# Strassen sums of a weight matrix made by accumulating DMAs instead of VectorE, in an FNet + gMLP block

## The chip, the cores and the metric

The kernel runs on one core of one Trainium2 chip. The metric is the device time of one execution in microseconds. Before the change three runs took 945.85 to 947.27 us, with a median of 946.61 us.

## The reference

The block is an FNet layer followed by a gMLP layer, on one sequence of 2048 rows and 512 columns, all in fp32. Cut to what matters:

```python
h = layernorm(x) * (1 + ca) + sa
a, b = h @ hid_re.T, h @ hid_im.T                   # 512 x 512
x = x + ga * (seq_re @ a - seq_im @ b)              # 2048 x 2048, twice
h = layernorm(x) * (1 + cb) + sb
z = gelu(h @ w_in)                                  # 512 x 1792
z1, z2 = z[..., :896], layernorm(z[..., 896:])
g = w_sp @ z2 + b_sp                                # 2048 x 2048
x = x + gb * ((z1 * g) @ w_out)                     # 896 x 512
```

The vectors `sa` to `gb` come from `silu(c) @ w_mod`. The change concerns the product with `w_sp` alone.

## The kernel before, in words

Every fp32 operand is split into a high and a low part, and every product is made as three TensorE matmuls (`matmul3`, lines 95 to 97: high by high, high by low, low by high). ScalarE makes a high part with one copy (`prep_hi`, line 256, tile `ah`), VectorE makes the low part with one subtraction (`prep_lo`, line 263, tile `al`). A unit `n` of the program is one 128 x 512 piece of a left-hand matrix, which TensorE multiplies in 12 matmuls. The pieces come in blocks of 512 x 512, four units to a block: SyncE issues four DMAs that load a block into `stage` (line 154, two buffers), and VectorE transposes it (line 227, tile `t`).

The program has these stages. Stage one is units 0 to 127: the two 2048 x 2048 DFT products, with the four groups of `mm_y` (tile `yp`) between the units, each of which ends in work on VectorE, GpSimd and ScalarE (`post_y`, `norm_y`, `post_h`). Then come 28 units for z1 (`N2` is 128, `N3` is 156), 16 units for z2, and 112 units (from `N4` on) for the product with `w_sp`; last the output product (`op`).

The product with `w_sp` is a Strassen-Winograd product with seven forms instead of eight, in the order 1, 6, 7, 4, 5, 3, 2 (`PROD`). Three of them read quarters of `w_sp` as they stand; the forms 5, 6, 7 and 3 read four sums of the quarters A11, A12, A21 and A22: S1 = A21 + A22, S2 = S1 - A11, S3 = A11 - A21 and S4 = A12 - S2. These are made ahead of time, piece by piece, during stage one and the z stages. A piece is loaded by SyncE into `sj` (line 756), VectorE makes the four sums in place (lines 761, 762, 765, 766), and GpSimd's queue stores them to `s_d` in HBM (line 769), from where the product's units load them like any other block (line 160).

The order on each engine is the order in which the program is written: `at(n, f, ...)` puts a call into the list of unit `n`, and `run(n)` calls the list after the unit's matmuls were written. Each engine, and each engine's DMA queue, runs its instructions in that order and waits at the first whose inputs or buffers are not ready. Line 1111 on places the pieces: 16 pieces of 128 rows by 512 columns in each of the four quarters, eight of them every five units from unit 85 on, each with its sums four and five units after its load; the other eight in the z stages. `sj` has two buffers in stage one (`spre0`, opened at unit 84) and four in the z stages. Just before unit 128 the pool that holds `spre0` is closed, and tiles of the z1 stage are put in its place, among them the weight sum `wt` (line 657).

GpSimd also holds, in the same queue, the loads of `xr` (line 544), the stores of `x_d` and `h_d` (lines 570 and 581) and the small arithmetic of the layer norm (lines 107, 108, 115), whose result ScalarE waits for in `norm_y` (line 119).

Of the kernel before, what the change touches and what calls it, by code (L numbers as in the profile page):

```python
# [19 lines left out]
def fnet_gmlp_kernel(  # L20
# [32 lines left out]
    nc = tc.nc  # L53
    S, D = x.shape[1:]
    F2 = w_in.shape[1]
    FH = F2 // 2
    Q = 512
# [18 lines left out]
    dram = ctx.enter_context(tc.tile_pool(name="dram", bufs=1, space=bass.MemoryType.DRAM))  # L76
    ctx.enter_context(tc.manual_schedule())

    def bank(k, name):
# [3 lines left out]
    h2_d = [dram.tile([Q, D], F32, name=f"h2_d{t}") for t in range(NQ)]  # L83
    z1_d = [dram.tile([NF, P, Q], F32, name=f"z1_d{t}") for t in range(NQ)]
    S_OF = {5: 1, 6: 2, 7: 3, 3: 4}
    s_d = {(m, r, g): dram.tile([Q, Q], F32, name=f"s_d{m}_{r}{g}")
           for m in range(1, 5) for r in range(2) for g in range(2)}
    def split(hi, lo, src):

        nc.scalar.activation(hi, src, AF.Copy)  # L90
        nc.vector.tensor_tensor(lo, src, hi.bitcast(F32), op=ALU.subtract)
# [31 lines left out]
    def at(n, f, *a):  # L123
        fill.setdefault(n, []).append((f, a))
# [6 lines left out]
    def quad(a, r, k):  # L131
        return a[r * Q:(r + 1) * Q, k * Q:(k + 1) * Q]
# [6 lines left out]
    N2 = 4 * len(src)  # L139
# [21 lines left out]

    def load(b):
        if b < len(src):
            stage[b] = blocks.tile([P, 16, P], F32, tag="stage", bufs=2, name=f"stage{b}")
            load_block(stage[b], src[b])
        elif b < len(src) + NQ * len(PROD):
            i, gh = divmod(b - len(src), NQ)
            g, h = divmod(gh, 2)
            p = PROD[i]
            stage[b] = blocks.tile([P, 2, 16, 64], F32, tag="stage", bufs=2, name=f"stage{b}")  # L170
            for r in range(2):
                load_half(stage[b][:, r], s_d[S_OF[p], r, g] if p in S_OF else
                          quad(w_sp, r + (2 if p == 4 else 0), g + (0 if p == 1 else 2)), h)

    def squares(dst, block, k):
# [26 lines left out]
    def turn_one(n, b0=0, b1=16):  # L202

        if b0 == 0:
            slot(n)
        squares(T[n][:, 32 * b0:32 * b1], stage[n % 2][:, b0:b1], n // 2)
        if n // 2 == 3 and b1 == 16:
            stage.pop(n % 2)
            if n % 2:
                load(3)  # L210
# [405 lines left out]
    def turn_z(t):  # L616
        b, q = N2 // 4 + t, t // 2
        if t == 1:
            ht = wpool[0].tile([P, 4, Q], F32, tag="wih", bufs=1, name="hz1")
        else:  # L620
            ht = spre[-1].tile([P, 4, Q], F32, tag="sj", bufs=4, name=f"hz{t}")
        st = stage.pop(b)
        for m in range(2):
            nc.vector.transpose(ht[:, 2 * m:2 * m + 2].rearrange("p k (b i) -> p k b i", i=32),
                                st[:, :, 64 * m:64 * m + 64].rearrange("p b (k i) -> p k b i", k=2))
        if t > 1:
            load(b + 2)
        if t % 2:
            RAW[q, 7], RAW[q, 4] = ht[:, :2], ht[:, 2:]
        else:  # L630
            RAW[q, 1] = RAW[q, 6] = ht[:, :2]
            RAW[q, 2] = RAW[q, 3] = ht[:, 2:]
# [114 lines left out]

    SJ = {}

    def load_s(r, g, b):  # L750

        SJ[r, g, b] = spre[-1].tile([P, 4, Q], F32, tag="sj", bufs=4 if len(spre) > 1 else 2, name=f"sj{r}{g}{b}")
        for i in range(2):
            v = w_sp.rearrange("(i r) (j c) -> i r j c", i=2, j=2)[i]
            o = r * Q + b * P
            nc.sync.dma_start(SJ[r, g, b][:, 2 * i:2 * i + 2], v[o:o + P][:, :, g * Q:(g + 1) * Q])

    def sum_s(r, g, b, first):
        a11, a12, a21, a22 = [SJ[r, g, b][:, i] for i in range(4)]
        if first:  # L760
            nc.vector.tensor_tensor(a22, a21, a22, op=ALU.add)  # L761
            nc.vector.tensor_tensor(a21, a11, a21, op=ALU.subtract)
            done = (1, a22), (3, a21)
        else:
            nc.vector.tensor_tensor(a11, a22, a11, op=ALU.subtract)
            nc.vector.tensor_tensor(a12, a12, a11, op=ALU.subtract)
            done = (2, a11), (4, a12)
        for m, a in done:
            nc.gpsimd.dma_start(s_d[m, r, g][b * P:(b + 1) * P, :], a)  # L769


    GW, UT, X2, OP, G, BH, BL = {}, {}, {}, {}, {}, {}, {}
# [12 lines left out]
    def b_of(p, k):  # L785
        return Z[k + 8 if p in (3, 2) else k][:, F2_ if p in (7, 5, 3) else F1]

    def hi_b(p, k):
        w = b_of(p, k).shape[-1]
        BH[p, k] = bpool[0].tile([P, Q], F32R, tag="bh", bufs=3, name=f"bh{p}_{k}")  # L790
        nc.scalar.activation(BH[p, k][:, :w], b_of(p, k), AF.Copy)  # L791

    def lo_b(p, k):
        w = b_of(p, k).shape[-1]
        BL[p, k] = bpool[0].tile([P, Q], F32R, tag="bl", bufs=3, name=f"bl{p}_{k}")
        nc.vector.tensor_tensor(BL[p, k][:, :w], b_of(p, k), BH[p, k][:, :w].bitcast(F32), op=ALU.subtract)

    def mm_w(n):
        i, m = divmod(n - N4, 4 * NQ)
# [204 lines left out]
    for s, n in ((8, 10), (9, 10)):  # L1004
        m = n + (s == 9)
# [23 lines left out]
    for j, turn, weigh, row, fold, hi in ((0, (25, 26, 27, 28), (29, 29, 30, 30), 26, (34, 34, 35, 36), (38, 35, 36, 37)),  # L1029
# [8 lines left out]
        n = weigh[3] + (3 if j == 0 else 1)  # L1038
# [21 lines left out]
    for t in range(NQ):  # L1060
        n = 8 * NQ * (t + 1)
# [35 lines left out]
    wpool, zpool, zrow, bpool, spre, gpool = [], [], [], [], [], []  # L1097
# [10 lines left out]
        spre.append(hp.enter_context(pool("spre0")))  # L1108

    at(84, change_q)  # L1110
    for i, u in enumerate((r, g, b) for g in range(2) for b in range(4) for r in range(2)):
        n = 85 + 5 * i if i < 8 else N2 + (13, 15, 28, 29, 31, 33, 35, 37)[i - 8]
        m = n + (4 if i < 8 or i > 9 else (9, 13)[i - 8])
        at(n, load_s, *u)
        at(m, sum_s, *u, True)
        at(m + 1, sum_s, *u, False)
    for n in range(N2):
        prep(n)
        mm_a(n)
# [25 lines left out]
    for i, p in enumerate(PROD):  # L1145
        for k in range(8):
            n = NB[p] + 2 * k
            at(n - 5, hi_b, p, k)
            at(n - 4, lo_b, p, k)
            if p == 1:  # L1150
                at(n + 3, sum_t23, k)
            if p == 4:
                at(n - 6, sum_t14, k)
# [33 lines left out]
    for f in range(NF):  # L1187
        n = NB[6] + 3 * f
# [66 lines left out]
```

## Time and profile before

| what | value |
|---|---|
| median of three runs | 946.61 us |
| span of the profiled execution, first to last instruction | 945.0 us |
| TensorE (PE) busy | 938.0 us, 99% of the span |
| VectorE (DVE) busy | 707.0 us, 75% |
| ScalarE (ACT) busy | 386.9 us, 41% |
| GpSimd (POOL) busy | 177.4 us, 19% |
| mean granted TensorE clock | 1.000 |
| bytes moved by DMA | 161.79 MB, 171 GB/s over the span |

The times in the profile are microseconds from the start of the span. The span is 1.6 us below the median of the runs, so a number that is worked out in the span is carried to the runs as a difference. SPq and ACTq are the queues (sequencers) of SyncE and ScalarE. In a row of a group, "x16 | 10.9, 680" means 16 instructions, 10.9 us in all, 680 ns each; what follows the second bar is the engine's idle time just before them and what ended it.

### The profile page before, as it was taken

How to read it: one execution, taken by the hardware profiler on the slowest of the kernel's cores; microseconds unless marked ns; L12 is line 12 of the kernel's file. 1: busy time of each engine (PE TensorE's matmuls, PEld its weight loads, DVE VectorE, ACT ScalarE, POOL GpSimd, SP SyncE). 2: the span in 40 equal slices, each digit the busy share in tenths (PEclk: the TensorE clock that was granted, in tenths of full speed). 3: DMA queues.
4: the chain of work that ended last, by engine and by line, in shares of the span. 5: the costliest groups of instructions: out<-in, count | busy, mean ns of one | idle time of the engine just before them, and what ended most of it. 6: DMA issues, size and time to landing. Idle time of an engine off the chain costs nothing.

```text
span 945.0 us, 12296 instructions
## 1 busy us (share of the span) xinstructions
PE 938.0 (99%) x4158; PEld 780.9 (83%) x4158; DVE 707.0 (75%) x1048; ACT 386.9 (41%) x670; POOL 177.4 (19%) x333
## 2 busy tenths in 40 slices
PE   8999999999999999999999999999999999999998
PEld 6878888888888888888888999888888888888886
DVE  7789957775765657767978587877688688885872
ACT  3685424232232222322876356544544444331221
POOL 1430000221631145122323265200000000000000
PEclk9999999999999999999999999999999999999999
DMA  8998653577668965996398985555554456833541
GB/s 194 222 214 165 130 134 90 146 197 158 134 101 197 281 208 150 279 281 141 95 344 282 326 267 160 149 114 134 124 134 90 106 117 141 205 107 117 198 155 59
DMA packets 253230, 161.79 MB, mean 171 GB/s; under 512 B 134576, under 2 KB 222896, under 8 KB 253040
## 3 DMA queue, kind: packets, MB, share of 16 engines
q1 hardware_dynamic: 238544, 120.62, 53.7%
q0 software_dynamic: 12272, 39.61, 12.3%
q10 hardware_dynamic: 2352, 0.79, 0.3%
q8 instruction: 32, 0.52, 0.3%
q14 instruction: 30, 0.25, 0.1%
HBM read 124.26 MB, written 36.71 MB: 170 GB/s over the span
## 4 chain that ended last, share of the span: by engine, by line
PE 94%; DMA 2%; SPq 1%; issue 1%; POOL 1%; DVE 0%; ACT 0%; ACTq 0%; DVEq 0%; POOLq 0%
PE gp L96 11%; PE gp L97 11%; PE gp L95 11%; PE gw L95 10%; PE gw L96 10%; PE gw L97 10%; PE yp L97 3%; PE yp L96 3%; PE yp L95 3%; PE z2p L96 3%; PE z2p L95 3%; PE z2p L97 3%; PE op L97 3%; PE op L95 3%; PE op L96 3%; PE z1p L96 1%
## 5 line engine op out<-in xcount | busy, mean ns | idle before, releaser
L256 ACT ACTIVATE ah<-t 128x512 fp32r<-128x512 f32 x263 | 164.4, 627 | 310.2 <-PE gp L97 181.0
L263 DVE TENSOR_TENSOR al<-t,ah 128x512 fp32r<-128x512 f32 x264 | 179.9, 685 | 133.4 <-PE gp L96 59.8
L96 PE MATMUL gp<-al,hh 128*128 128x512 f32 x480 | 186.8, 389 | 1.2 <-DVE al L263 1.2
L97 PE MATMUL gp<-ah,hl 128*128 128x512 f32 x480 | 186.8, 389 | 0.0
L95 PE MATMUL gp<-ah,hh 128*128 128x512 f32 x480 | 186.7, 389 | 0.0
L97 PE MATMUL gw<-ah,bl 128*128 128x512 f32 x400 | 155.6, 389 | 0.0
L96 PE MATMUL gw<-al,bh 128*128 128x512 f32 x400 | 155.6, 389 | 0.0
L95 PE MATMUL gw<-ah,bh 128*128 128x512 f32 x400 | 155.6, 389 | 0.0
L96 PEld LDWEIGHTS gp<-al,hh 128*128 128x128 f32 x480 | 90.1, 188 | 20.4 <-DVE al L263 1.6
L95 PEld LDWEIGHTS gp<-ah,hh 128*128 128x128 f32 x480 | 90.1, 188 | 18.7
L97 PEld LDWEIGHTS gp<-ah,hl 128*128 128x128 f32 x480 | 90.1, 188 | 18.8 <-DVE hl L448 0.2
L97 PEld LDWEIGHTS gw<-ah,bl 128*128 128x128 f32 x400 | 75.1, 188 | 15.7
L95 PEld LDWEIGHTS gw<-ah,bh 128*128 128x128 f32 x400 | 75.1, 188 | 15.5
L96 PEld LDWEIGHTS gw<-al,bh 128*128 128x128 f32 x400 | 75.1, 188 | 15.5
L227 DVE STREAM_TRANSPOSE t<-stage 128x1024 f32<-128x1024 f32 x62 | 76.7, 1238 | 8.7 <-DMA stage<-in_A_dft_seq_re_dram 8.6
L221 DVE STREAM_TRANSPOSE t<-stage 128x1024 f32<-128x1024 f32 x56 | 69.3, 1238 | 0.1
L791 ACT ACTIVATE bh<-z 128x512 fp32r<-128x512 f32 (+1 forms) x56 | 32.8, 586 | 65.7 <-PE gw L96 65.7
L769 POOL DMA_DIRECT2D s_d<-sj x64 | 35.1, 550 | 107.5 <-DVE sj L761 80.7
L95 PE MATMUL yp<-hth,gh 128*128 128x512 f32 x128 | 49.8, 389 | 0.0
L96 PE MATMUL yp<-htl,gh 128*128 128x512 f32 x128 | 49.8, 389 | 0.0
L97 PE MATMUL yp<-hth,gl 128*128 128x512 f32 x128 | 49.8, 389 | 0.0
L96 PE MATMUL z2p<-wil,ah 128*128 128x448 f32 x128 | 46.7, 365 | 0.0
(210 smaller groups left out, 1448.0 us busy)
## 6 DMA issues: line engine op xcount, KB each, us to landing
sj<-in_B_w_sp_dram SPq DMA_DIRECT2D x32, 512.0 KB, 8.3
s_d<-sj POOLq DMA_DIRECT2D x64, 256.0 KB, 4.1
stage<-s_d SPq DMA_DIRECT2D x128, 128.0 KB, 2.9
stage<-in_A_dft_seq_re_dram SPq DMA_DIRECT2D x60, 256.0 KB, 5.4
stage<-in_A_dft_seq_im_dram SPq DMA_DIRECT2D x60, 256.0 KB, 5.9
stage<-in_B_w_sp_dram SPq DMA_DIRECT2D x96, 128.0 KB, 3.1
stage<-h_d SPq DMA_DIRECT2D x32, 256.0 KB, 6.4
xr<-in_A_x_dram POOLq DMA_DIRECT2D x16, 256.0 KB, 4.3
```

What stands on the lines that cost most here:

```text
L95: nc.tensor.matmul(acc, ah, bh, start=first, stop=False, skip_group_check=go_on)
L96: nc.tensor.matmul(acc, ah, bl, start=False, stop=False, skip_group_check=go_on)
L97: nc.tensor.matmul(acc, al, bh, start=False, stop=last, skip_group_check=go_on)
L221: nc.vector.transpose(t.rearrange("p r (b i) -> p r b i", i=32), st[:, :, :, 16 * k:16 * k + 32])
L227: nc.vector.transpose(t.rearrange("p k (b i) -> p k b i", i=32), st[:, :, 32 * k:32 * k + 64].rearrange("p b (k i) -> p k b i", k=2))
L256: nc.scalar.activation(AH[n], source(n), AF.Copy)
L263: nc.vector.tensor_tensor(AL[n], source(n), AH[n].bitcast(F32), op=ALU.subtract)
L769: nc.gpsimd.dma_start(s_d[m, r, g][b * P:(b + 1) * P, :], a)
L791: nc.scalar.activation(BH[p, k][:, :w], b_of(p, k), AF.Copy)
```

## The change

The four sums are no longer made by VectorE. The pieces become 8 strips of 128 rows by 2048 columns in each half of `w_sp`, and every sum is made by DMAs, some of which add what they carry to what lies at their destination:

1. SyncE loads the strip's lower rows (A21 and A22) into `sj`, 1 MB, and copies A12 from `w_sp` in HBM to the place of S4 in HBM, 512 KB (`load_s`).
2. ScalarE negates both halves of `sj`; GpSimd's queue stores -A21 to the place of S1 (`negate_s`).
3. GpSimd's queue adds -A22 to S1 in HBM, and adds A11 from HBM to -A21 in `sj`, which becomes S3 (`sum_s1`).
4. It stores S3, and adds S3 to -A22 within `sj`, which becomes -S2 (`sum_s2`).
5. It stores -S2, and adds -S2 to the A12 in the place of S4 (`sum_s4`).

S1 and S2 are held with the opposite sign, so the products 5 and 6 take the negative of their other operand: `hi_b` copies with a scale of -1, and `lo_b` becomes one `scalar_tensor_tensor`. The first six strips are placed every six units from unit 85 on, with their steps four, six, eight and ten units after the load; the last two lie in the z stages.

```diff
-    s_d = {(m, r, g): dram.tile([Q, Q], F32, name=f"s_d{m}_{r}{g}")
-           for m in range(1, 5) for r in range(2) for g in range(2)}
+    s_d = {(m, r): dram.tile([Q, 2 * Q], F32, name=f"s_d{m}_{r}") for m in range(1, 5) for r in range(2)}
...
-    def load_s(r, g, b):
-        SJ[r, g, b] = spre[-1].tile([P, 4, Q], F32, tag="sj", bufs=4 if len(spre) > 1 else 2, name=f"sj{r}{g}{b}")
-        for i in range(2):
-            v = w_sp.rearrange("(i r) (j c) -> i r j c", i=2, j=2)[i]
-            o = r * Q + b * P
-            nc.sync.dma_start(SJ[r, g, b][:, 2 * i:2 * i + 2], v[o:o + P][:, :, g * Q:(g + 1) * Q])
-
-    def sum_s(r, g, b, first):
-        a11, a12, a21, a22 = [SJ[r, g, b][:, i] for i in range(4)]
-        if first:
-            nc.vector.tensor_tensor(a22, a21, a22, op=ALU.add)
-            nc.vector.tensor_tensor(a21, a11, a21, op=ALU.subtract)
-            done = (1, a22), (3, a21)
-        else:
-            nc.vector.tensor_tensor(a11, a22, a11, op=ALU.subtract)
-            nc.vector.tensor_tensor(a12, a12, a11, op=ALU.subtract)
-            done = (2, a11), (4, a12)
-        for m, a in done:
-            nc.gpsimd.dma_start(s_d[m, r, g][b * P:(b + 1) * P, :], a)
+    def s_rows(m, b):
+        return s_d[m, b // 4][b % 4 * P:(b % 4 + 1) * P, :]
+
+    def load_s(b):
+        SJ[b] = spre[-1].tile([P, 2, 2 * Q], F32, tag="sj", bufs=4 if len(spre) > 1 else 2, name=f"sj{b}")
+        nc.sync.dma_start(SJ[b], w_sp[S // 2 + b * P:S // 2 + (b + 1) * P, :].rearrange("p (j c) -> p j c", j=2))
+        nc.sync.dma_start(s_rows(4, b), w_sp[b * P:(b + 1) * P, 2 * Q:])
+
+    def negate_s(b):
+        for j in range(2):
+            nc.scalar.activation(SJ[b][:, j], SJ[b][:, j], AF.Copy, scale=-1.0)
+        nc.gpsimd.dma_start(s_rows(1, b), SJ[b][:, 0])
+
+    def sum_s1(b):
+        nc.gpsimd.dma_start(s_rows(1, b), SJ[b][:, 1], accum_op=ALU.add)
+        nc.gpsimd.dma_start(SJ[b][:, 0], w_sp[b * P:(b + 1) * P, :2 * Q], accum_op=ALU.add)
+
+    def sum_s2(b):
+        nc.gpsimd.dma_start(s_rows(3, b), SJ[b][:, 0])
+        nc.gpsimd.dma_start(SJ[b][:, 1], SJ[b][:, 0], accum_op=ALU.add)
+
+    def sum_s4(b):
+        nc.gpsimd.dma_start(s_rows(2, b), SJ[b][:, 1])
+        nc.gpsimd.dma_start(s_rows(4, b), SJ[b][:, 1], accum_op=ALU.add)
...
-        nc.scalar.activation(BH[p, k][:, :w], b_of(p, k), AF.Copy)
+        nc.scalar.activation(BH[p, k][:, :w], b_of(p, k), AF.Copy, scale=-1.0 if p in (5, 6) else 1.0)
...
-        nc.vector.tensor_tensor(BL[p, k][:, :w], b_of(p, k), BH[p, k][:, :w].bitcast(F32), op=ALU.subtract)
+        hi = BH[p, k][:, :w].bitcast(F32)
+        if p in (5, 6):
+            nc.vector.scalar_tensor_tensor(BL[p, k][:, :w], b_of(p, k), -1.0, hi, op0=ALU.mult, op1=ALU.subtract)
+        else:
+            nc.vector.tensor_tensor(BL[p, k][:, :w], b_of(p, k), hi, op=ALU.subtract)
...
-    for i, u in enumerate((r, g, b) for g in range(2) for b in range(4) for r in range(2)):
-        n = 85 + 5 * i if i < 8 else N2 + (13, 15, 28, 29, 31, 33, 35, 37)[i - 8]
-        m = n + (4 if i < 8 or i > 9 else (9, 13)[i - 8])
-        at(n, load_s, *u)
-        at(m, sum_s, *u, True)
-        at(m + 1, sum_s, *u, False)
+    for b in range(8):
+        n = 85 + 6 * b if b < 6 else N2 + (16, 20)[b - 6]
+        m = n + 4 if b < 6 else N2 + (28, 31)[b - 6]
+        at(n, load_s, b)
+        at(m, negate_s, b)
+        at(m + 2, sum_s1, b)
+        at(m + 4, sum_s2, b)
+        at(m + 6, sum_s4, b)
```

What the change moves is seen best on three queues. On GpSimd, before, from the first piece on: four stores of one piece (`sj_2733` is its buffer), a load of `xr`, and the four stores of the next.

```order
L769 DMA s_d_00_88<-sj_2733 128x512
L769 DMA s_d_00_96<-sj_2733 128x512
L769 DMA s_d_00_92<-sj_2733 128x512
L769 DMA s_d_00_100<-sj_2733 128x512
L544 DMA xr_0_2895<-in_A_x_dram 128x512
L769 DMA s_d_10_90<-sj_2842 128x512
```

The same place now, with the whole of the first strip (`sj_2725`): the rows of lines 765, 766, 770 and 774 are the four that add.

```order
L762 DMA s_d_0_88<-sj_2725 128x1024
L765 DMA s_d_0_88<-sj_2725 128x1024
L766 DMA sj_2725<-in_B_w_sp_dram 128x1024
L543 DMA xr_0_2884<-in_A_x_dram 128x512
L769 DMA s_d_0_92<-sj_2725 128x1024
L770 DMA sj_2725<-sj_2725 128x1024
L773 DMA s_d_0_90<-sj_2725 128x1024
L774 DMA s_d_0_94<-sj_2725 128x1024
L762 DMA s_d_0_88<-sj_2847 128x1024
```

Before, the stores of a piece read only what VectorE had made. Now line 765 adds to what line 762 stored, line 769 and line 770 read what line 766 made, and lines 773 and 774 read what line 770 made: each must wait for an earlier DMA of the same queue to land, and what stands behind it waits with it.

On ScalarE, now, around the negation of the strip with index 5 (`sj_3553`), which is placed at unit 119; before, this place held `ah` rows alone.

```order
L255 ACTIVATE ah_3601<-t_3558 128x512
L255 ACTIVATE ah_3617<-t_3594 128x512
L761 ACTIVATE sj_3553<-sj_3553 128x1024 x2
L255 ACTIVATE ah_3640<-t_3594 128x512
L255 ACTIVATE ah_3656<-t_3638 128x512
```

The row `ah_3640` is the high part for unit 123. ScalarE comes to it only when the strip has been loaded and negated.

On SyncE, now, from the third strip on. Every strip's load is one row of 1 MB and one copy from HBM to HBM of 512 KB, and its place between the loads of `stage` is fixed; before, there were two loads of 512 KB at each such place.

```order
L755 DMA sj_3015<-in_B_w_sp_dram 128x2048
L756 DMA s_d_0_94<-in_B_w_sp_dram 128x1024
L153 DMA stage_3022<-in_A_dft_seq_re_dram 32x16x128 x4
L153 DMA stage_3160<-in_A_dft_seq_im_dram 32x16x128 x4
L755 DMA sj_3229<-in_B_w_sp_dram 128x2048
L756 DMA s_d_0_94<-in_B_w_sp_dram 128x1024
```

The third strip takes the first strip's buffer, so its row waits until the last row of the first strip on GpSimd (line 774) has landed, and the four rows of `stage` behind it wait with it.

More of the change, by code (lines that the diff above doesn't have):

```diff
@@ L171, in load @@
             for r in range(2):
-                load_half(stage[b][:, r], s_d[S_OF[p], r, g] if p in S_OF else
+                load_half(stage[b][:, r], s_d[S_OF[p], r][:, g * Q:(g + 1) * Q] if p in S_OF else
                           quad(w_sp, r + (2 if p == 4 else 0), g + (0 if p == 1 else 2)), h)
```

## The prediction

> **What bounds the kernel now.** I read the engines' totals first, then what TensorE waited for, then the long middle of the span by itself.
>
> ```profile
> span 945.0 us, 12296 instructions
> PE 938.0 (99%) x4158; PEld 780.9 (83%) x4158; DVE 707.0 (75%) x1048; ACT 386.9 (41%) x670; POOL 177.4 (19%) x333
> ...
> engine line waited for: us in total, times, longest us
> PE busyp L349 <- DVE busy L284: 1.5, 1, 1.5
> PE gp L96 <- DVE al L263: 1.2, 1, 1.2
> PE gp L468 <- DVE ah L959: 0.9, 1, 0.9
> ...
> 75.00:925.00 850.00, 850.00 (x3791) 711.16 (x3790) 643.20 (x941) 338.26 (x572) 155.38 (x265) 1.00 0.64 170
> ```
>
> The last row is a window of 850 us: its columns are the length, then busy time and count of PE, PEld, DVE, ACT and POOL, the granted clock, the DMA share and GB/s. TensorE was busy in all 850 us, at a granted clock of 1.00. Its waits in the whole span sum to 3.6 us, all in the first 75 us, which the change does not touch. So between 75 and 925 us no other engine's work costs time as long as it is in time, and VectorE, busy in 643 of these 850 us, holds TensorE up nowhere. A saving on VectorE can therefore give nothing. The whole question is whether the new work is ever late.
>
> **What goes away.** The sums on VectorE:
>
> ```profile
> L766 DVE TENSOR_TENSOR sj<-sj 128x512 f32<-128x512 f32 x16 | 12.0, 753 | 0.6
> L762 DVE TENSOR_TENSOR sj<-sj 128x512 f32<-128x512 f32 x16 | 12.0, 752 | 0.6
> L761 DVE TENSOR_TENSOR sj<-sj 128x512 f32<-128x512 f32 x16 | 10.9, 680 | 1.7 <-DMA sj<-in_B_w_sp_dram 1.7
> L765 DVE TENSOR_TENSOR sj<-sj 128x512 f32<-128x512 f32 x16 | 10.6, 663 | 0.0
> ...
> L528 DVE SCALAR_TENSOR_TENSOR ht<-ht,col,w 128x512 f32<-128x512 f32 x8 | 5.7, 729 | 0.0
> ...
> L796 DVE TENSOR_TENSOR bl<-z,bh 128x512 fp32r<-128x512 f32 x32 | 20.9, 652 | 0.0
> ```
>
> That is 64 instructions and 45.5 us of VectorE, worth 0 us of the span by the window above. The 16 `lo_b` of the products 5 and 6 become another form: the nearest row, 729 ns, against 652 ns makes at most 16 x 0.08 = 1.2 us on an engine with a quarter of its time free, and I take 0.
>
> **What comes onto ScalarE.** Sixteen negations of 128 x 1024. The nearest rows:
>
> ```profile
> L668 ACT ACTIVATE wh<-wraw 128x1024 fp32r<-128x1024 f32 x3 | 3.2, 1056 | 1.9 <-DMA wraw<-in_B_w_in_dram 1.5 <-DVE wraw L657 0.4
> ...
> 401.20 0.63 ACT L256 ACTIVATE ah<-t 128x512 fp32r<-128x512 f32 x1 [2.08 <-PE gp L97]
> 403.93 0.63 ACT L256 ACTIVATE ah<-t 128x512 fp32r<-128x512 f32 x1 [2.10 <-PE gp L97]
> ...
> 412.08 0.63 ACT L256 ACTIVATE ah<-t 128x512 fp32r<-128x512 f32 x1 [2.08 <-PE gp L97]
> ```
>
> 2 x 1.06 = 2.1 us a strip, against idle times of 2.1 us before each `ah`: the work itself is hidden. What is not cheap is the wait in front of it. ScalarE makes `ah` for unit n + 3 at unit n and is let on by TensorE's end of unit n - 1. With the row at 401.20 (unit 119) four units ahead of the row at 412.08, TensorE can go on until 412.1 us with what ScalarE has made before the negation placed at unit 119. After that it stands still until the strip has landed, been negated and the next `ah` (0.63 us) is made.
>
> **What comes onto the DMA engines.** This is the part that can hurt. Before, a piece had a load of 2 x 512 KB and four stores of 256 KB. Its price, and what the DMA engines reach:
>
> ```profile
> sj<-in_B_w_sp_dram SPq DMA_DIRECT2D x32, 512.0 KB, 8.3
> s_d<-sj POOLq DMA_DIRECT2D x64, 256.0 KB, 4.1
> ...
> 300.00:325.00 25.00, 25.00 (x112) 20.70 (x111) 17.95 (x24) 7.97 (x13) 4.79 (x9) 1.00 0.88 273
> 325.00:350.00 25.00, 25.00 (x112) 20.69 (x111) 15.62 (x23) 5.26 (x8) 11.05 (x18) 1.00 0.71 201
> 350.00:375.00 25.00, 25.00 (x112) 20.71 (x111) 14.95 (x23) 4.85 (x8) 9.43 (x15) 1.00 0.69 190
> 375.00:400.00 25.00, 25.00 (x112) 20.71 (x111) 19.99 (x27) 7.98 (x13) 6.59 (x10) 1.00 0.86 259
> 400.00:425.00 25.00, 25.00 (x112) 20.67 (x112) 16.69 (x24) 6.94 (x12) 6.49 (x12) 1.00 0.98 269
> ...
> 475.00:500.00 25.00, 25.00 (x112) 20.71 (x111) 19.51 (x25) 18.20 (x30) 5.37 (x10) 1.00 1.08 351
> ```
>
> In the stretch where the sums are made the DMA engines are busy 0.69 to 0.98 of the time already, at a mean of 238 GB/s. The most that any window shows is 351 GB/s, with a share above 1; I take that as what they can do.
>
> Now the size of a slot. The first sums of the pieces at units 89, 119 and 124 started here:
>
> ```profile
> 298.25 0.69 DVE L761 TENSOR_TENSOR sj<-sj 128x512 f32<-128x512 f32 x1
> ...
> 401.61 0.68 DVE L761 TENSOR_TENSOR sj<-sj 128x512 f32<-128x512 f32 x1
> ...
> 416.37 0.65 DVE L761 TENSOR_TENSOR sj<-sj 128x512 f32<-128x512 f32 x1
> ```
>
> The strips stand six units apart, so 30 units in 103.4 us make 20.7 us a strip. Before, a piece every (416.37 - 298.25) / 7 = 16.9 us moved 1.05 MB in and 1.05 MB out, so 2.6 MB in 20.7 us. All traffic in 20.7 us was 238 x 20.7 = 4.9 MB; what is left for `stage` and the rest is 2.3 MB. Now a strip moves 1.05 MB (load) and eight times 0.52 MB (one copy, three stores, four additions), 5.2 MB. With the 2.3 MB it is 7.5 MB, and 7.5 MB / 351 GB/s = 21.4 us, if an adding DMA costs what a plain one costs. An addition has to fetch what lies at its destination too; if these bytes count in full, 4 x 0.52 = 2.1 MB more, it is 9.6 / 351 = 27.4 us. No row of this trace shows a DMA that adds, so 21.4 and 27.4 us are the two ends for the period P of a strip. I take P = 25 us, nearer the upper end: the bytes have to be fetched, but 351 GB/s was reached with many short rows of `stage` in it. The slot of 20.7 us is too short for any of them; the strips fall behind by P - 20.7 each.
>
> By the Trainium skill, page "Collectives: The Full Stack", Part 3, an addition in the DMA costs no cycles by itself but needs two source reads, so a reduction runs at about half the rate of a copy; no run here shows it yet. By it the sum below would go with 27.4 us, and it is a rival of its own.
>
> **Where being late reaches TensorE.** Two places.
>
> Strip 5 takes the buffer of strip 3. Strip 0 is negated from 298.25 on and its first store goes out at 300.4 us; strip b's at 300.4 + bP. The last addition of strip 3 stands just ahead of strip 4's first store, 300.4 + 4P, and lands later by some 8.3 us (the row of a 512 KB transfer); then strip 5's load can start and lands another 8.3 us later: 317.0 + 4P. ScalarE then needs 2.1 + 0.6 us for the negations and the `ah`. TensorE stands still by 317.0 + 4P + 2.7 - 412.1 = 4P - 92.4 us. At 25 us: **7.6 us**. At 21.4: nothing. It begins at P = 23.1.
>
> The second is the tile that is put over `sj` just before the z1 stage:
>
> ```profile
> 453.60 0.96 DVE L657 TENSOR_TENSOR wt<-wraw,wraw 128x768 f32<-128x768 f32 x1
> ```
>
> It must wait for the last addition of strip 5, 300.4 + 6P + 8.3 us; before, the last store had landed long ago. At 25 us that is 458.7, or 5.1 us late, which the 7.6 us lost by then cover. At 27.4 us it is 473.1, 19.5 us late, and then this place counts instead of the first (17.2).
>
> SyncE's `stage` rows behind a waiting strip load are late too: strip 5's load starts at 300.4 + 100 + 8.3 = 408.7 us, some 7 us after unit 119. A block is loaded six units, 16 us, before VectorE takes it, and the profile gives the landing of such a load below; I take 0 for this, but without that cover it is the first to follow.
>
> ```profile
> stage<-in_A_dft_seq_im_dram SPq DMA_DIRECT2D x60, 256.0 KB, 5.9
> ```
>
> The last two strips lie in the z stages, two units apart with 24 matmuls each, so with more room, and the sums are read from 600 us on: 0. The sum: 945.0 + 7.6 = 952.6 us of span, and with the 1.6 us between the span and the median, **954.2 us**.
>
> **Rivals.** *The additions cost as much as plain copies.* Then P is 21.4 us, under the 23.1 from which ScalarE's negation decides, TensorE never waits, and the time is 946.6 us: not slower. For it: stores of 256 KB land in 4.1 us even here. Against it: the DMA share of 0.98 leaves no room for 1.5 times the bytes. *They cost two copies in full* (the rule above): P = 27.4, 19.5 us at the tile `wt`, 966 us. *They cost three or more*: 7.5 + 2 x 2.1 = 11.7 MB, P = 33.3; strip 5 is done at 300.4 + 200 + 8.3 = 508.7 us, 55 us after `wt` was due, about 1002 us. Nothing in the trace excludes it. *Faster*: VectorE's free 45 us shorten one of the waits of 3.6 us. They lie before 75 us and the sums after 298, so only a faster clock or tail could do it: 944 us.
>
> **How the numbers follow.** A measurement of this kernel tells a change of about 0.2%, 1.9 us. Chances: the forecast, a stall of 2 to 14 us, 0.36; additions as cheap as copies 0.28; two copies 0.20; three or more 0.13; faster 0.03. So faster 0.03, same 0.28, slower 0.69. The range that leaves out the dearest case and the faster one goes from 945.5 to 985; the forecast's own is 948 to 961.
>
> **What would show it.** In the changed profile TensorE has waits between 400 and 470 us, released by ScalarE's `ah` or, at 454 us and later, by what follows `wt`; ScalarE is idle before the negations, released by the load of `sj`; the first stores of the strips stand about 25 us apart; the DMA share between 300 and 425 us is at or above 1. The first step is wrong if TensorE waits anywhere the strips are not in play. The sum is wrong if the period is under 23 us or over 28 us, and the forecast is wrong in kind if the strips keep to 20.7 us.

## The result, and the profile after

The changed kernel takes **998.25 us** (median of four runs, 995.31 to 1000.14) against 946.85 us for the kernel before beside it: slower by 5.4%, ratio 1.0541 with a 95% interval of 1.0522 to 1.056. Ratios, here and below, leave out two runs at twice the time and more, which no trace explains: 1930.86 us, one of four of a kernel below, and 2448.39 us, one of the kernel before. The profiled execution has a span of 993.5 us, 48.5 us more than before.

The engines' totals, and the two largest groups of what TensorE waited for (us in total, times, longest), in the kernel after:

```profile
span 993.5 us, 12172 instructions
PE 948.7 (95%) x4158; PEld 786.1 (79%) x4158; DVE 669.4 (67%) x984; ACT 400.4 (40%) x686; POOL 176.5 (18%) x325
...
PE yp L94 <- DVE y L567: 21.7, 1, 21.7
PE gp L94 <- ACT ah L255: 13.2, 2, 9.9
```

VectorE is relieved by 37.6 us (707.0 to 669.4), and TensorE waits 41.4 us in sum instead of 3.6. So 37.8 us of the 48.5 are new waits. TensorE is also busy for 10.7 us more with the same 4158 matmuls. The windows of the kernel after show why (length; busy time and count of PE, PEld, DVE, ACT, POOL; granted clock, DMA share, GB/s):

```profile
375.00:400.00 25.00, 19.48 (x67) 14.77 (x66) 12.55 (x15) 7.36 (x12) 10.74 (x15) 0.80 0.96 261
400.00:425.00 25.00, 22.29 (x97) 17.76 (x95) 7.56 (x9) 3.68 (x7) 3.42 (x5) 1.00 1.01 226
425.00:450.00 25.00, 16.85 (x65) 13.51 (x66) 10.40 (x14) 9.00 (x14) 3.98 (x6) 0.80 1.08 246
450.00:475.00 25.00, 15.36 (x68) 12.39 (x66) 2.38 (x4) 0.00 (x0) 5.85 (x10) 0.86 0.93 239
475.00:500.00 25.00, 12.93 (x47) 10.52 (x48) 16.96 (x24) 6.91 (x10) 11.21 (x18) 0.67 0.52 135
...
386.00:396.00 10.00, 8.04 (x18) 5.88 (x19) 8.52 (x9) 3.73 (x7) 5.58 (x7) 0.50 0.87 244
396.00:426.50 30.50, 26.29 (x114) 21.02 (x113) 9.41 (x11) 5.46 (x8) 3.76 (x6) 1.00 0.99 227
```

All the loss but 0.5 us lies between 375 and 500 us. The granted clock falls to 0.50 after a stop of TensorE: between 386 and 396 us it is busy 8.04 us for only 18 matmuls. From 375 to 475 us the DMA engines are full (share 0.93 to 1.08), yet move 226 to 261 GB/s and not the 351 that I had taken as their ceiling.

Where TensorE stood still is seen on the engines ahead of it. Rows of ScalarE and VectorE after (start, duration; in brackets the idle time before and its releaser):

```profile
383.79 0.81 ACT L118 ACTIVATE h<-xr,nmry,rsy 128x512 f32<-128x512 f32 x1 [10.49 <-POOL nmry L114]
...
430.57 2.00 ACT L761 ACTIVATE sj<-sj 128x1024 f32<-128x1024 f32 x2 [15.60 <-DMA sj<-in_B_w_sp_dram]
...
483.39 0.81 ACT L118 ACTIVATE h<-xr,nmry,rsy 128x512 f32<-128x512 f32 x1 [33.72 <-POOL nmry L114]
...
473.67 0.69 DVE L568 TENSOR_TENSOR xr<-y,xr 128x512 f32<-128x512 f32 x1 [18.46 <-DMA xr<-in_A_x_dram]
```

The row at 430.57 is the negation of strip 5, the first place that the prediction named: ScalarE idled 15.6 us for the strip's load, and TensorE 9.9 us, until 433.15, for the `ah` behind it. The other rows are something else: ScalarE waits for `nmry`, a small row of GpSimd, and VectorE for a load of `xr` that GpSimd issues. GpSimd's queue, in the kernel after:

```profile
299.58 0.54 POOL L762 DMA_DIRECT2D s_d<-sj  x1 [19.54 <-ACT sj L761]
...
450.27 0.89 POOL L762 DMA_DIRECT2D s_d<-sj  x1
464.45 0.84 POOL L765 DMA_DIRECT2D s_d<-sj  x1 [13.29 <-DMA s_d<-sj]
...
465.56 1.81 POOL L543 DMA_DIRECT2D xr<-in_A_x_dram  x2
473.21 0.54 POOL L769 DMA_DIRECT2D s_d<-sj  x1 [5.84 <-DMA sj<-in_B_w_sp_dram]
...
480.07 0.55 POOL L773 DMA_DIRECT2D s_d<-sj  x1 [4.30 <-DMA sj<-sj]
480.60 0.94 POOL L774 DMA_DIRECT2D s_d<-sj  x1
481.17 0.92 POOL L569 DMA_DIRECT2D x_d<-xr  x1
```

The first stores (line 762) of strips 0 and 5 stand (450.27 - 299.58) / 5 = **30.1 us** apart. Behind the last row of strip 5 comes the store `x_d` of the last group of stage one, at 481.17, and then that group's norm rows. In the kernel before the same store went out at 432.79:

```profile
432.79 0.54 POOL L570 DMA_DIRECT2D x_d<-xr  x1 [12.04 <-DVE xr L569]
```

It is 48.4 us late, and the span is 48.5 us longer.

### The profile page after: what moved, and what is told of

Same layout as the page of the kernel before. It is cut to its first block, busy times and chain, and to the rows that moved or that the text cites. A ratio compares the mean times of both kernels' runs of the same rounds, so it can differ in the third digit from the quotient of the medians.

```text
span 993.5 us, 12172 instructions
## 1 busy us (share of the span) xinstructions
PE 948.7 (95%) x4158; PEld 786.1 (79%) x4158; DVE 669.4 (67%) x984; ACT 400.4 (40%) x686; POOL 176.5 (18%) x325
## 2 busy tenths in 40 slices
DMA packets 249774, 170.17 MB, mean 171 GB/s; under 512 B 134192, under 2 KB 222512, under 8 KB 248560
## 4 chain that ended last, share of the span: by engine, by line
PE 49%; DVE 1%; issue 0%; ACT 0%; DVEq 0%
PE gw L94 9%; PE gw L96 9%; PE gw L95 9%; PE z2p L95 3%; PE z2p L94 3%; PE z2p L96 3%; PE op L96 3%; PE op L95 3%; PE op L94 3%; PE z1p L95 1%; PE z1g L94 1%; PE z1p L96 1%; PE z1g L95 1%; PE z1g L96 1%; PE z1p L94 1%
## 5 line engine op out<-in xcount | busy, mean ns | idle before, releaser
L262 DVE TENSOR_TENSOR al<-t,ah 128x512 fp32r<-128x512 f32 x264 | 184.7, 703 | 169.7 <-PE gp L95 59.9
L94 PE MATMUL gp<-ah,hh 128*128 128x512 f32 x480 | 189.3, 394 | 15.1 <-ACT ah L255 13.2
L95 PE MATMUL gp<-al,hh 128*128 128x512 f32 x480 | 189.5, 395 | 2.5 <-DVE al L262 2.5
L96 PE MATMUL gp<-ah,hl 128*128 128x512 f32 x480 | 188.9, 393 | 0.0
L95 PEld LDWEIGHTS gw<-al,bh 128*128 128x128 f32 x400 | 75.1, 188 | 15.6
L94 PE MATMUL z2p<-wih,ah 128*128 128x448 f32 x128 | 46.7, 365 | 0.0
```

Of the source, the lines that this page charges most:

```text
L94: nc.tensor.matmul(acc, ah, bh, start=first, stop=False, skip_group_check=go_on)
L95: nc.tensor.matmul(acc, ah, bl, start=False, stop=False, skip_group_check=go_on)
L96: nc.tensor.matmul(acc, al, bh, start=False, stop=last, skip_group_check=go_on)
L262: nc.vector.tensor_tensor(AL[n], source(n), AH[n].bitcast(F32), op=ALU.subtract)
```

## The experiments

I first asked what makes a strip take 30.1 us, then which place sets the time, and last whether the additions cost anything where no one stands behind them. A time without a ratio is that of a single run; a period is the distance of the first stores of strips 0 and 5 in its profile, divided by 5.

### All eight transfers plain

The four additions become copies, so the sums are left out; one of the four edits:

```diff
-        nc.gpsimd.dma_start(s_rows(1, b), SJ[b][:, 1], accum_op=ALU.add)
+        nc.gpsimd.dma_start(s_rows(1, b), SJ[b][:, 1])
...
```

> All 32 adding DMAs become plain copies of the same bytes; every wait stays, and the four sums are left out of the result. In the changed kernel a strip takes 30.1 us from first store to first store, and the adding DMAs land 6 to 12 us after issue. Theory A (an addition loads the DMA engines about like two copies, and that sets the strip's period): the period falls to 22 us or less, and the span to 945 to 955 us. Theory B (the period is the sum of the landings that GpSimd's queue waits for one after the other, whatever the DMAs do): the period stays at 28 us or more and the span above 980 us.

Measured: 967.53 us, span 965.5, period 25.8 us. Neither expectation held. Adding accounts for 30.1 - 25.8 = 4.3 us of a strip; 20.5 us of the 48.5 stay without any addition. The landings of the strip's transfers of 512 KB between 300 and 480 us (issues; KB; median us to landing), first of the kernel after, then of this one:

```profile
sj<-in_B_w_sp_dram POOLq DMA_DIRECT2D x6, 512.0 KB, 11.5
sj<-sj POOLq DMA_DIRECT2D x6, 512.0 KB, 9.8
```

```profile
sj<-in_B_w_sp_dram POOLq DMA_DIRECT2D x6, 512.0 KB, 9.0
sj<-sj POOLq DMA_DIRECT2D x6, 512.0 KB, 7.4
```

An addition lands 2.4 or 2.5 us later than a copy on the same path, at about the same DMA share. The copies' 9.0 and 7.4 us are already far above the 4.1 us of the stores before, which carried half as much (256 KB).

### Half of the additions plain

```diff
-        nc.gpsimd.dma_start(s_rows(1, b), SJ[b][:, 1], accum_op=ALU.add)
+        nc.gpsimd.dma_start(s_rows(1, b), SJ[b][:, 1])
...
-        nc.gpsimd.dma_start(s_rows(4, b), SJ[b][:, 1], accum_op=ALU.add)
+        nc.gpsimd.dma_start(s_rows(4, b), SJ[b][:, 1])
```

> Only the additions into HBM (S1 and S4, lines 765 and 774) become plain copies; S1 and S4 are left without their second term. Nothing on GpSimd's queue waits for these two directly, except the next load of the strip's buffer. Theory A: half of the extra load goes, the period falls from 30.1 to about 26 us and the span to about 965 us. Theory B: the period stays within 1 us of 30 and the span above 985 us.

> Only the additions into the SBUF tile (lines 766 and 770) become plain copies, so S2, S3 and S4 are not the sums. These two are the ones that the next row of GpSimd's queue waits for. Theory A: as with the additions into HBM, about 26 us a strip and about 965 us of span. If the additions on the chain count for more than those beside it: 24 us or less, and a span under 960 us. Theory B: 28 us or more.

The first makes the two transfers into HBM plain (the diff above), the second, in the same way, the two into `sj` (lines 766 and 770); the sums concerned are left out. Measured: 981.7 us with a period of 27.8, and 986.37 us with 28.8. So 2.3 us of a strip go with the additions into HBM and 1.3 with those into `sj`: both kinds cost, in sum 3.6 of the 4.3 us of the run before, and neither makes up the whole by itself.

### The last group's `xr` loaded early

The loads of `xr` for the last group, which the trace showed to be late by 18.46 us, go out at unit 116, ahead of strip 5.

```diff
-            if i < 2:
+            if t == NQ - 1:
+                at(116, load_xr, t, i)
+            elif i < 2:
...
-            elif i == 0:
-                for j in range(2, 4):
-                    at(y - 2, load_xr, t, j)
```

> The four loads of xr for the last group of stage one are placed at unit 116, ahead of the last strip's rows on GpSimd; all sums are made. In the changed kernel TensorE waits 21.7 us for VectorE's y of that group, which waits for xr. If that place alone costs the time: the wait of 21.7 us goes and with it the half clock there, and the span falls by 22 us or more, to 970 us or less. If the tile wt, which is put over the strip's buffer, is next in line: it can be written only when the last addition has landed (486.7 us in the changed kernel), so a new wait of about 10 us stands at the start of z1, and the span falls by 8 to 14 us, to about 980 to 985 us.

Measured: 999.42 us. Both expectations missed, and this was the run that taught most. `xr` was there in time (VectorE used it at 458.98 us, not at 473.67), and nothing was gained; ScalarE in this kernel:

```profile
487.57 0.81 ACT L118 ACTIVATE h<-xr,nmry,rsy 128x512 f32<-128x512 f32 x1 [32.89 <-POOL nmry L114]
```

The norm rows behind `x_d` stand in the same queue behind the same strip. It is not one load that is late, it is all of GpSimd's queue behind the last strip. With that I compared the `x_d` row in every kernel; the table stands below.

### Two chains that overlap a little

Line 774 of a strip and line 762 of the next stood in that order, so each strip began only when the last row of the one before had gone out. Here the last step of the first six strips comes one unit later, which puts the next strip's first store ahead of it.

```diff
-        at(m + 6, sum_s4, b)
+        at(m + (7 if b < 6 else 6), sum_s4, b)
```

> The change with the last step of each of the first six strips one unit later, so that on GpSimd's queue the next strip's first store stands ahead of the last two rows of the strip before it, and the two chains overlap a little. All bytes and additions are the same. Theory A (a strip's 30.1 us are mostly the chain of landings on GpSimd's in-order queue, 11.5 + 9.8 + 7.1 us and the landing of the first store): the period of the first stores falls to 23 to 27 us and the time to 955 to 980 us. Theory B (the DMA engines' bytes set the 30.1 us: share 0.98 to 1.08 at about 250 GB/s): the period stays at 29 to 31 us, the landings get longer, and the time is 992 to 1004 us.

Measured: 974.63 us; the first stores, of strips 0 and 5:

```profile
300.54 0.54 POOL L762 DMA_DIRECT2D s_d<-sj  x1 [19.53 <-ACT sj L761]
...
425.60 0.56 POOL L762 DMA_DIRECT2D s_d<-sj  x1 [1.97 <-ACT sj L761]
```

The period is 25.0 us with the same bytes and all additions. So 5.1 of the 30.1 us were time in which a strip waited for its own landings while the queue held the next strip back: the chain theory held. The first store of strip 5 now waits for ScalarE's negation and no longer for the queue. Both changes together, order and no adding:

> The changed kernel without the adding (all eight transfers of a strip are plain copies, so the sums are left out), and with the last step of the first six strips one unit later, as in the run before this one that had the additions. If the chain of landings (30.1 to 25.0 us a strip by that order) and the additions (30.1 to 25.8 us a strip by leaving the adding out) are two prices that add up, both together give 30.1 - 5.1 - 4.3 = 20.7 us, the slot itself: periods of 20.5 to 22 us, and 945.5 to 952 us. If both are the same thing, bytes at the DMA engines' limit, the period stays at 24 to 26 us and the time at 962 to 972 us.

```profile
299.35 0.54 POOL L762 DMA_DIRECT2D s_d<-sj  x1 [19.53 <-ACT sj L761]
...
408.91 0.53 POOL L762 DMA_DIRECT2D s_d<-sj  x1 [2.60 <-ACT sj L761]
...
407.56 2.01 ACT L761 ACTIVATE sj<-sj 128x1024 f32<-128x1024 f32 x2 [6.10 <-DMA sj<-in_B_w_sp_dram]
...
400.00:425.00 25.00, 25.00 (x112) 20.71 (x111) 11.87 (x16) 8.95 (x14) 4.82 (x9) 1.00 1.06 341
```

Measured: 956.84 us, period 21.9 us, up to 341 GB/s. The period fell into the range of the adding-up theory, the time stayed 5 us above it: the slot is 20.7 us, and the row of `x_d` behind the strips is 10.2 us late (table below). What sets the 21.9 us is not shown to be bytes: the negation of strip 5 waits 6.10 us for its load, which went out at 402.01, behind the last row (394.09) of strip 3, whose buffer it takes. The two prices overlap a little: 30.1 - 21.9 = 8.2 us, not 9.4. In this order adding costs 25.0 - 21.9 = 3.1 us a strip.

### VectorE's relief, and the negated operands, alone

The kernel before without the 64 sums (the pieces are stored as loaded, so the sums are left out):

```diff
-            nc.vector.tensor_tensor(a22, a21, a22, op=ALU.add)
-            nc.vector.tensor_tensor(a21, a11, a21, op=ALU.subtract)
...
-            nc.vector.tensor_tensor(a11, a22, a11, op=ALU.subtract)
-            nc.vector.tensor_tensor(a12, a12, a11, op=ALU.subtract)
```

> The kernel before with the 64 sums on VectorE left out (the pieces are stored as they are loaded, so the product with w_sp is of other numbers): what the relief of VectorE by 45.5 us is worth by itself. Theory (0 us, since TensorE does not wait between 75 and 925 us): within 0.2% of before, 945 to 948 us. Rival: VectorE's relief lets something ahead of TensorE be earlier, the 3.6 us of waits go in part: 942 to 944.5 us.

Measured: 946.92 us, ratio 1.0001 (0.9991 to 1.001), with 40 us less of VectorE:

```profile
75.00:925.00 850.00, 850.00 (x3791) 711.22 (x3790) 603.33 (x876) 340.25 (x574) 148.70 (x265) 1.00 0.64 170
```

The kernel before with the signs of the change alone, the sums still on VectorE:

```diff
-            nc.vector.tensor_tensor(a22, a21, a22, op=ALU.add)
+            nc.vector.scalar_tensor_tensor(a22, a21, -1.0, a22, op0=ALU.mult, op1=ALU.subtract)
...
+        if p in (5, 6):
+            nc.vector.scalar_tensor_tensor(BL[p, k][:, :w], b_of(p, k), -1.0, hi, op0=ALU.mult, op1=ALU.subtract)
```

> The kernel before with one part of the change alone: S1 and S2 are held with the opposite sign (VectorE still makes the sums, one of the four as a scalar_tensor_tensor) and the products 5 and 6 take negated operands. Theory (what the prediction took, 0): 16 low parts at 0.08 us more and 16 sums in another form on an engine with a quarter of its time free; within 0.2% of before, 945 to 948.5 us, no wait of TensorE after 75 us. Rival: the other form of lo_b is late at a change of product and costs 16 x 0.08 = 1.3 us or more, 948 to 950 us.

Measured: 946.72 us, ratio 0.9998 (0.9989 to 1.0007). Both parts are worth nothing that these runs can tell, as the prediction took them.

### Five strips in stage one

```diff
-    for b in range(8):
-        n = 85 + 6 * b if b < 6 else N2 + (16, 20)[b - 6]
-        m = n + 4 if b < 6 else N2 + (28, 31)[b - 6]
+    for b, (n, m, *steps) in enumerate(
+            [(n, n + 4, n + 6, n + 8, n + 10) for n in (85, 91, 97, 103, 109)] +
+            [tuple(N2 + k for k in u) for u in ((13, 23, 24, 29, 31), (15, 24, 25, 30, 34), (28, 34, 37, 39, 41))]):
...
```

> The changed kernel with the same pitch of six units, but five strips in stage one instead of six; the sixth is made in the z stages, with the placing of the run beside this one. Theory A (the row of x_d of the last group on GpSimd, behind the last strip of stage one, sets the time): the last addition of strip 4 goes out where strip 5's first store was in the change, about 450 us, so x_d goes out at 450.5 +- 3 us, 17.7 us late, and the time is 961 to 968 us. Theory B (the two places that the prediction named, ScalarE's negation of strip 5 and wt over the buffers): there is no strip 5 left in stage one and strip 4's last addition lands at about 457 us, 3 us after wt is due: 946 to 951 us.

Measured: 979.65 us, outside both. The queue shows what I had left out:

```profile
457.12 0.55 POOL L773 DMA_DIRECT2D s_d<-sj  x1 [11.12 <-DMA sj<-sj]
457.66 0.89 POOL L774 DMA_DIRECT2D s_d<-sj  x1
458.21 2.54 POOL L543 DMA_DIRECT2D xr<-in_A_x_dram  x4
465.51 0.55 POOL L569 DMA_DIRECT2D x_d<-xr  x1 [4.76 <-DVE xr L568]
```

Strip 4 ended 7 us later than I had put it, and the loads of `xr` now stood behind it too, 7.3 us more before `x_d`. The theory's number was wrong by 15 us. But `x_d` is 32.7 us late and the span 32.9 us longer: the place is the queue and not strip 5's negation, since there is no strip 5 in stage one here; `wt` alone would have made 946 to 951 us. All kernels with strips, by that row:

| kernel | `x_d` of the last group, us | later than before | span longer by |
|---|---|---|---|
| the change | 481.17 | 48.4 | 48.5 |
| all transfers plain | 453.64 | 20.9 | 20.5 |
| plain into HBM | 467.87 | 35.1 | 34.8 |
| plain into `sj` | 472.21 | 39.4 | 39.4 |
| `xr` early | 485.36 | 52.6 | 52.6 |
| overlapped | 460.55 | 27.8 | 27.8 |
| overlapped, plain | 442.98 | 10.2 | 9.9 |
| five strips | 465.51 | 32.7 | 32.9 |

In eight kernels the two differ by at most 0.4 us: from that row on, all need the same time to the end, so what they lose lies ahead of it. That GpSimd's queue is what holds the row back, and not a late TensorE, is seen in the rows: it goes out right behind line 774, or waits (4.76 us with five strips) for an `xr` whose load stood in the same queue.

### Four strips in stage one, four behind it

The last question: do the additions cost TensorE anything where nothing waits behind them? Four placements, all with every addition; the steps are load, negation, and lines 765, 769 and 773.

```diff
...
+            [(85 + 9 * b, 89 + 9 * b, 91 + 9 * b, 94 + 9 * b, 97 + 9 * b) for b in range(4)] +
+            [tuple(N2 + k for k in u) for u in ((13, 23, 26, 28, 30), (15, 28, 30, 32, 34), (28, 33, 35, 37, 39),
+                                                (29, 36, 38, 40, 42))]):
...
```

> The change with four strips in stage one, nine units (31 us at 3.45 us a unit) apart instead of six strips six units (20.7 us) apart, and four strips spread over the z stages; every sum is still made by additions. Theory A (the rate in stage one is the cause: a strip of this change needs 30.1 us and was given 20.7): strips 0 to 3 keep to their places within 5 us, the row of x_d of the last group on GpSimd, 48.4 us late in the change, is at most 3 us late, TensorE's waits fall from 41.4 us to under 8, and the time is 946 to 952 us. Theory B (an adding strip disturbs wherever it lies, by its chain of landings or its bytes): the lateness moves into the z stages, TensorE waits there by 10 us or more, and the time is 958 to 985 us.

Measured: 966.27 us, ratio 1.0201 (1.0177 to 1.0224). The time and the wait are those that theory B had forecast. In stage one GpSimd's queue was in time (`x_d` at 433.18, 0.4 us late), but the strips' bytes met the loads of the weight `wraw`, which landed in 11.8 us in the median and not in 7.6 as before: ScalarE waited for one, and TensorE then lost 3.4 us in three short waits. In the z stages the norm rows of z stood behind a strip's wait, and TensorE waited 10.6 us for what ScalarE made of them.

```profile
440.35 1.06 ACT L667 ACTIVATE wh<-wraw 128x1024 fp32r<-128x1024 f32 x1 [4.37 <-DMA wraw<-in_B_w_in_dram]
...
559.46 0.56 POOL L769 DMA_DIRECT2D s_d<-sj  x1 [11.29 <-DMA sj<-in_B_w_sp_dram]
...
561.89 0.26 POOL L114 TENSOR_SCALAR nmrz<-mvz,rsz 128x1 f32<-128x1 f32 x1
```

In the kernel before, the first `nmrz` row stood here:

```profile
540.74 0.27 POOL L115 TENSOR_SCALAR nmrz<-mvz,rsz 128x1 f32<-128x1 f32 x1
```

The second placement set the steps further apart.

```diff
...
+            [(n, n + 4, n + 6, n + 10, n + 14) for n in (85, 94, 103, 111)] +
+            [tuple(N2 + k for k in u) for u in ((13, 17, 18, 23, 28), (15, 21, 22, 29, 31), (28, 31, 34, 38, 42),
+                                                (29, 34, 35, 39, 43))]):
...
```

> All eight strips and all their additions, four strips in stage one and four in the z stages, with the steps of a strip placed a landing (10 to 12 us) or more apart, and never in front of small rows of GpSimd that TensorE's next work hangs on (x_d and the norm rows of the last group in stage one, nmrz in the z stages). Theory A (the slowdown is nothing but rows of GpSimd's queue that stand behind a strip's wait for a landing; the additions by themselves cost TensorE nothing): the x_d row of the last group goes out at 432.8 +- 1 us, the row of nmrz is no more than 2 us late, and the time is 945.5 to 949 us. Theory B (the bytes of the additions cost TensorE time wherever they lie, through late loads of stage): 952 to 966 us, with waits released by al or ah that wait for stage.

Measured: 972.19 us, ratio 1.0269 (1.0241 to 1.0298), outside both. `x_d` went out at 432.89, but the loads of `wraw` were late again (TensorE lost 3.8 us), and I had put a negation ahead of its load's landing, and ScalarE stood in front of it as at the prediction's first place:

```profile
504.29 2.00 ACT L761 ACTIVATE sj<-sj 128x1024 f32<-128x1024 f32 x2 [8.94 <-DMA sj<-in_B_w_sp_dram]
...
511.48 0.79 PE L94 MATMUL z1g<-ah,w 128*128 128x512 f32 x1 [8.71 <-ACT z1k L695]
```

The first `nmrz` was late too, at 558.88, behind a wait of GpSimd's queue of 16.62 us for line 770's landing. The third mended the negation, and ended the strips of stage one earlier, so that they met no load of `wraw` (7.2 us to land).

```diff
...
+            [(n, n + 4, n + 6, n + 9, n + 12) for n in (85, 92, 100, 107)] +
+            [tuple(N2 + k for k in u) for u in ((13, 23, 24, 29, 31), (15, 24, 25, 30, 34), (28, 34, 37, 39, 41),
+                                                (29, 35, 38, 41, 43))]):
...
```

> All eight strips and all their additions, once more spread four and four, now with what the run before it showed mended: the strips of stage one end earlier (loads at units 85, 92, 100 and 107), so that the loads of wraw at 425 us meet no strip; in the z stages the negations stand ten units or nine after their load for the first two strips and six for the last two (the load had landed 10 us after its negation's place, and ScalarE waited 8.9 us), and no step of a strip stands ahead of a group of nmrz rows unless its transfer has landed. Theory A (every loss so far is a queue that stands behind a strip's landing, and the additions themselves cost TensorE nothing): no wait of TensorE over 2 us after 75 us, 945.5 to 951 us. Theory B (the bytes cost time wherever they lie): the losses come back elsewhere, 955 to 972 us.

Measured: 957.64 us, ratio 1.0108 (1.0092 to 1.0125). Outside theory A's range once more and inside theory B's, but with a single place left: the first `nmrz` at 551.50, 10.8 us late, and a span 11.5 us longer.

```profile
549.06 0.55 POOL L773 DMA_DIRECT2D s_d<-sj  x1 [6.91 <-DMA sj<-sj]
...
551.50 0.27 POOL L114 TENSOR_SCALAR nmrz<-mvz,rsz 128x1 f32<-128x1 f32 x1
```

The fourth takes that place away.

```diff
-            [tuple(N2 + k for k in u) for u in ((13, 23, 24, 29, 31), (15, 24, 25, 30, 34), (28, 34, 37, 39, 41),
-                                                (29, 35, 38, 41, 43))]):
+            [tuple(N2 + k for k in u) for u in ((13, 23, 24, 28, 31), (15, 28, 30, 34, 38), (28, 35, 37, 40, 42),
+                                                (29, 37, 38, 41, 43))]):
```

> All eight strips and all their additions as in the run before (four in stage one, at units 85, 92, 100 and 107), with only the steps of the four strips of the z stages moved so that no step waits for a landing ahead of a group of nmrz rows. Theory A (only the rows behind a strip's landing cost time): the first nmrz goes out at 541 +- 2 us, TensorE has no wait over 1.5 us after 75 us, and the time is 945.5 to 949 us, the same as before to 0.3%. Theory B (the bytes of the additions cost TensorE time by themselves): the 11.5 us of the run before come back in another place, 953 us or more.

Measured: **947.35 us** against 946.73, ratio 1.0001 (0.9988 to 1.0013), with every sum still made by additions. Its waits of TensorE, the two rows of GpSimd, and the window of 850 us that bounded the kernel before:

```profile
PE busyp L348 <- DVE busy L283: 1.5, 1, 1.5
PE gp L95 <- DVE al L262: 1.1, 1, 1.1
PE gp L467 <- DVE ah L968: 0.7, 1, 0.7
...
432.61 0.55 POOL L569 DMA_DIRECT2D x_d<-xr  x1 [13.78 <-DVE xr L568]
...
540.79 0.27 POOL L114 TENSOR_SCALAR nmrz<-mvz,rsz 128x1 f32<-128x1 f32 x1
...
75.00:925.00 850.00, 850.00 (x3790) 711.13 (x3790) 603.30 (x876) 352.69 (x587) 156.38 (x257) 1.00 0.71 180
```

Both rows stand where they stood before, and TensorE waits nowhere after the first 75 us. In this placement the additions and their bytes cost TensorE nothing that these runs can tell. What cost in the change was a queue that stood behind their landings; bytes alone cost 3.4 and 3.8 us where they met `wraw`. The kernel is as fast as the kernel before and not faster, which is what a relief of an engine off the bound is worth.

## Why the prediction was wrong

**Right.** TensorE bounds the kernel, and what VectorE is relieved of is worth 0: measured 946.92 us without the sums (45.5 us by the lengths of their rows; VectorE's busy time fell by 40). `lo_b` and the signs are worth 0: 946.72. The question was whether the new work is late, and it was. ScalarE's negation hurts by the wait in front of it: 15.60 us of idle time at 430.57, TensorE 9.9. The DMA share was about 1 as told (0.96 to 1.04). SyncE's `stage` rows, taken as 0, were late, but cost little: VectorE idled 6.87 us for one until 410.36, and TensorE 0.93 us at 412.23. The second place, `wt`, never decided: VectorE came to it only at 502.26, behind the late rows of the last group.

**Wrong: the period P.** I took 25 us, with ends of 21.4 and 27.4; it was 30.1. The price of adding was about right: the 25 held 3.6 us for it (6.0 at the upper end), and it costs 3.1 to 4.3. The Trainium skill's "Collectives: The Full Stack", Part 3, has a ring's reduction run at about half the rate of its copy; taken as the price of adding here, as the 27.4 us took it, it is too high. What was missing is a term of its own: on GpSimd's queue a strip's steps wait for landings of 9.8 and 11.5 us, and the next strip may not start meanwhile, 3.9 (25.8 - 21.9, plain) to 5.1 us a strip. I had named that order in the section on the change, and costed the bytes alone. The term of plain bytes, 21.4 us, is near the 21.9 us of plain copies whose chains overlap, but that is no proof of it: the windows from 300 to 425 us moved 321 GB/s there in the mean, not 351, and strip 5 waited 6.10 us for its load.

**Wrong: the places.** I listed ScalarE's negation and `wt`, and never asked what GpSimd's rows behind strip 5 hold up; that wait stands in the sum as nothing. The prediction's own formula puts the last row of strip 5 at 300.4 + 6P. With P = 25 that is 450.4 us, and `x_d`, due at 432.79, is 17.6 us late: 964 us, not 954.2. With P = 30.1 it is 481.0, 48.2 late: 994.8 us. So of the 44 us between 954.2 and 998.25 us, the missing place makes 10 and the period 31; about 3 us lie between the profiled execution and the median. This holds for strips that follow one another: in the overlapped order P was 25.0 us, but a strip took longer than its period, and `x_d` was 27.8 us late and not 17.6.

**Wrong in kind: a rival that had nearly the right number.** "Three or more copies" gave 1002 us, by additions of 11.9 us a strip. They cost about a third of that. Its time fits for another reason, and its mechanism did not occur.

**Not thought of: the granted clock.** TensorE's stops of 3.24 us and more are followed by half clock. Where the strips' chain sets the time, this costs nothing more, as the table shows; where a single stop sets it, it does: in the third placement above, a stop of 7.2 us was followed by a window at 0.50,

```profile
558.00:568.00 10.00, 5.92 (x16) 5.27 (x17) 6.94 (x15) 9.60 (x16) 4.24 (x9) 0.50 1.10 288
```

in which 5.92 us of busy time held 16 matmuls; in the kernel before, 52 filled these 10 us, so 16 take about 3.

## What to carry to other kernels

Moving work from a free engine to DMAs that read each other's results moves it into an in-order queue: list what stands behind each such row, up to the row that the bounding engine's work hangs on, and compute when that row goes out. The lateness of that one row equalled the whole slowdown in eight kernels. A chain of dependent transfers needs its landings as well as its bytes in the sum. In the last placement, with nothing urgent behind the steps and no urgent load beside them, the same transfers cost nothing that could be measured.

## What the runs showed of the hardware that I had not expected

- Adding lowers what the DMA engines move at about the same share: 257, 260, 278, 261 and 226 GB/s in the five windows from 300 to 425 us after (shares 0.96 to 1.04), 263, 329, 325, 302 and 267 with plain transfers (0.86 to 1.03). That is 256 against 297 GB/s in the mean. The profile counts the same 170.17 MB for both kernels, so its bytes do not tell an addition from a copy.
- TensorE's clock. Rows of it after (in brackets the stop ahead of a matmul):

```profile
385.18 0.49 PE L94 MATMUL gp<-ah,hh 128*128 128x512 f32 x1 [3.24 <-ACT ah L255]
...
390.45 0.79 PE L94 MATMUL gp<-ah,hh 128*128 128x512 f32 x1 [1.96 <-DVE gl L90]
412.23 0.50 PE L95 MATMUL gp<-al,hh 128*128 128x512 f32 x1 [0.93 <-DVE al L262]
```

  The stop of 3.24 us was followed by a granted clock of 0.50 until 396 us; the one of 0.93 us was not, since the window from 396 to 426.5 us above has 1.00. The Trainium skill, "TensorE: Matmul & The Clock Gate", Part 1, has the clock halved after an idle window of about 3.4 us and back after about as long a busy one. The stop of 3.24 us is a little shorter than that and was still followed by half clock; the full rate came back 3.9 us after the end of the stop of 9.93 us, 4.6 us after that of 21.71 us and 5.7 us after that of 1.96 us, so somewhat later than the figure.
- With the DMA share near 1, even plain transfers of 512 KB within SBUF take 7.4 us to land, in the median between 300 and 480 us.
- What else is in flight is slowed with them: between 300 and 425 us the 256 KB loads of `stage` from the two DFT matrices landed in 5.4 and 5.3 us in the median before, and in 12.2 and 12.9 us after.
